# Moving stage four of the first two batches within their slots, in a Fourier-mixing and mixture-of-experts kernel

## The chip, the cores and the metric

The kernel runs on one core of a Trainium2 chip. The metric is the device time of one execution in microseconds; for the kernel before it is the median of three runs, 1559.63 us (1558.89 to 1561.95). A profiled execution of the same kernel spans 1579.1 us; all readings of the profile below are on that scale.

## The reference

Two blocks follow each other. The first takes 8 batches of 2496 tokens of 256 channels through a real Fourier transform along the tokens, multiplies by a complex filter and transforms back. The second sends each of the 19968 resulting tokens to the one of 8 experts with the highest gate logit; an expert is two matrix products with a relu between.

```python
X = np.fft.rfft(x, axis=1)
Y = X * (filt_r + 1j * filt_i)[None]
x = np.fft.irfft(Y, n=2496, axis=1).reshape(19968, 256)

logits = x @ w_gate
expert_idx = np.argmax(logits, axis=1)
gate_w = softmax(logits)[row, expert_idx]
for e in range(8):                      # rows of expert e
    h = np.maximum(x[rows] @ w1[e], 0.0)
    y[rows] = h @ w2[e]
out = gate_w[:, None] * y
```

## The kernel before

The length 2496 is 39 times 64, so each batch's transform is four products with small matrices: stage A (39 points, L342), stage B (64 points, L356) with the filter after it, stage C (64 points back, L382) and stage D (39 points back, L401 and L405), which is stage four. Between A and B, and between C and D, a batch goes through DRAM (`zd`, `ud`), as the axes change; only batch 0 stays on the chip and is turned by TensorE transposes instead. After D a batch is transposed (`turn_y`, L476), the logits are computed (L490) and transposed (L501), and a routing chain of small VectorE instructions finds the expert and the row of each token; GpSimd then scatters the rows to DRAM (L617). Once a batch is routed, a chain of small VectorE instructions (`tile_map`, L636 to L688) lists the expert tiles that are now full. Their work (transposes L750, first product L793 or L834, second product L851) fills the gaps between the Fourier steps.

The host program lays all steps of a slot on a scale from 0 to about 1 and emits them in that order; `slot(k)` has stages B and C of batch k, stage A of batch k + 1 and stage D with the routing of batch k - 1:

```python
def slot(k):
    steps, nch = [], len(CH)                       # nch = 6 chunks of up to 4 columns
    ...                                            # k == 0: batch 0 on the chip
    elif k < B:
        for f in range(0, NF + 4, 2):              # NF = 20
            at = f / (NF + 4)
            if f < NF:
                steps.append((at, lambda f=f: stage_b(k, f), ("z", k, f // 4) if f % 4 == 0 else None, 0.85))
            if f >= 4:
                steps.append((at + 0.01, lambda f=f: stage_c(k, f - 4), None, 0.85))
    if k + 1 < B:
        for c in range(nch):
            steps.append(((0.25 if k == 0 else 0.0) + 0.7 * c / nch, lambda c=c: stage_a(k + 1, c), ("x", k + 1, c), 0.43 * CH[c][1]))
    if k > 0:
        for c in range(nch + 3):
            at = 0.45 * c / (nch + 3) - 0.1 if k == 1 else 0.2 + 0.8 * c / (nch + 3)
            if c < nch and k == 1:
                steps.append((at - 0.05, lambda c=c: turn_u(c), None, 0.22 * CH[c][1]))
            if c < nch:
                steps.append((at, lambda c=c: stage_d(k - 1, c), ("u", k - 1, c) if k > 1 else "y", 0.43 * CH[c][1]))
            if c >= 3 and c % 2:
                steps.append((at + 0.01, lambda c=c: logits(k - 1, (c - 3) // 2), None, 0.9))
            if 1 <= c <= nch:
                steps.append((at + 0.03, lambda c=c: turn_y(k - 1, c - 1), None, 0.22 * CH[c - 1][1]))
            if c >= 3 and c % 2:
                later = at + (0.07 if k == 1 else 0.11)
                steps.append((later, lambda c=c: turn_logits(k - 1), None, 0.25))
                steps.append((later + 0.001, lambda c=c: sides.append(route(k - 1, (c - 3) // 2)), None, 0.0))
            if k == 1 and c == nch:
                steps.append((at, experts_pool, None, 0.0))
        steps.append((0.38 if k == 1 else 2.0, lambda: begin_route(k - 1), None, 0.0))
    return sorted(steps, key=lambda step: step[0])
```

`begin_route` appends the batch's tile map to `sides`, a queue of small work of which some instructions are emitted after each step. Stage B's multiplications by the filter are on VectorE; their final sum is on GpSimd for the first batches as long as `sides` is empty, else on VectorE:

```python
nc.vector.tensor_mul(ys, z2, ht[:, f:f + 2, :])                                   # L363
nc.vector.scalar_tensor_tensor(out=yw[:HP], in0=z2[HP:], scalar=-1.0, in1=fi, ...)  # L364
nc.vector.tensor_mul(yw[HP:], z2[:HP], fi)                                        # L365
if b == 0 or b < 3 and not sides:
    nc.gpsimd.tensor_tensor(ys, ys, yw, op=ALU.add)                               # L369
else:
    nc.vector.tensor_tensor(ys, ys, yw, op=ALU.add)                               # L372
```

Results in PSUM are evicted by VectorE or ScalarE (L228), whichever the host's own bookkeeping has free earlier. The routing chain has one instruction on ScalarE, the exponential (L527), in the midst of those on VectorE. All loads and stores other than the scatters are issued by SyncE, in the order in which they are emitted; inputs of the stages (`fin`) have 7 buffers, outputs that go to DRAM (`zo`, `uo`) share 4. A load of `u` is emitted once all of the batch's stage C is, and waits for its stores.

Of the kernel before, what the change touches and what calls it, by code (L numbers as in the profile page):

```python
# [118 lines left out]
def kernel(  # L119
# [216 lines left out]
    def stage_a(b, c):  # L336
        i0, n = CH[c]
        xt = ins.pop(("x", b, c))
        zo = sb.tile([TK, 4, D], F32, tag="st", name="zo", bufs=4)
        for j in range(0, n, 2):  # L340
            p = bank()
            mm(p[:TK, :], lhsT=tas, rhs=xt[:TP, j:j + 2, :], start=True, stop=True)  # L342
            evac(zo[:, j:j + 2, :], p[:TK, :].rearrange("p (t d) -> p t d", t=2), 512)
        for r, m, v in columns(zd[b], i0, n):
            move(v, zo[:r, m])
        if c == len(CH) - 1:
            mark(("a", b))

    def stage_b(b, f):
        c, j = divmod(f, 4)  # L350
        if b == 0:
            zi, j = outs.pop(("zi", f)), 0
        else:
            zi = ins["z", b, c] if j == 0 else ins.pop(("z", b, c))
        p = bank()
        mm(p, lhsT=tbs, rhs=zi[:, j:j + 2, :], start=True, stop=True)  # L356

        z2 = p.rearrange("p (i d) -> p i d", i=2)
        ys = outs["y", b, f] = sb.tile([P, 2, D], F32, tag="ys", name="ys", bufs=4)
        yw = (pro if b == 0 else sb).tile([P, 2, D], F32, tag="yw", name="yw", bufs=2)  # L360
        half, f1 = divmod(f, NF // 2)
        fi = ht[half * HP:(half + 1) * HP, NF + f1:NF + f1 + 2, :]
        nc.vector.tensor_mul(ys, z2, ht[:, f:f + 2, :])  # L363
        nc.vector.scalar_tensor_tensor(out=yw[:HP], in0=z2[HP:], scalar=-1.0, in1=fi, op0=ALU.mult, op1=ALU.mult)  # L364
        nc.vector.tensor_mul(yw[HP:], z2[:HP], fi)  # L365
        free["v"] = max(free["v"], now[0]) + 2.1

        if b == 0 or b < 3 and not sides:
            nc.gpsimd.tensor_tensor(ys, ys, yw, op=ALU.add)  # L369
            free["p"] = max(free["p"], free["v"]) + (1.4 if b else 0.0)  # L370
        else:
            nc.vector.tensor_tensor(ys, ys, yw, op=ALU.add)  # L372
            free["v"] += 0.7

    def stage_c(b, f):
        ys = outs.pop(("y", b, f))
        j = f % 4
        if j == 0:
            outs["u", b] = sb.tile([P, 4, D], F32, tag="st", name="uo", bufs=4)
        uo = outs["u", b]  # L380
        p = bank()
        mm(p, lhsT=tcs, rhs=ys, start=True, stop=True)  # L382
        evac(uo[:, j:j + 2, :], p.rearrange("p (i d) -> p i d", i=2), 512)
        if j == 2:
            f0 = f - 2
            move(ud[b][:, f0:f0 + 4, :], uo[:HP])
            move(ud[b][:, NF + f0:NF + f0 + 4, :], uo[HP:])
        if f == NF - 2:
            mark(("c", b))
# [42 lines left out]
    def turn_z(f):  # L432
        if f % 4 == 0:
            nc.scalar.copy(out=ht[HP:, f:f + 4], in_=ht[:HP, f:f + 4])
            free["s"] = max(free["s"], now[0]) + 1.1
        zi = outs["zi", f] = pro.tile([P, 2, D], F32, tag="zi", name="zi")
        p = bank().rearrange("p (i h d) -> p i h d", i=2, h=DH)
        for i in range(2):
            for h in range(DH):
                nc.tensor.transpose(p[:, i, h, :], zu["z"][:, h, f + i].rearrange("p c t -> p (c t)"), ident)  # L440
        evac(zi, p.rearrange("p i h d -> p i (h d)"), 2 * D)

    def first_c(f):
        ys = outs.pop(("y", 0, f))
        p = bank().rearrange("p (h i c t) -> p h i c t", h=DH, c=2, i=2)
        for i in range(2):
            for h in range(DH):
                mm(p[:, h, i].rearrange("p c t -> p (c t)"), lhsT=ys[:, i, h * P:(h + 1) * P],
                   rhs=tcs, start=True, stop=True)
        for h in range(DH):  # L450
            evac(zu["u"][:, h, :, :, f:f + 2], p[:, h].rearrange("p i c t -> p t c i"), D)

    def turn_u(c):
        i0, n = CH[c]
        ui = outs["ui", c] = pro.tile([P, 4, D], F32, tag="ui", name="ui")
        for j in range(0, n, 2):
            p = bank().rearrange("p (i h d) -> p i h d", i=2, h=DH)
            whole = i0 + j + 2 < NG
            for i in range(2):
                t0 = NB * (i0 + j + i)  # L460
                m = min(NB, N2 - t0)
                for h in range(DH):
                    nc.tensor.transpose(
                        p[:m * NS, i, h, :], zu["u"][:, h, t0:t0 + m].rearrange("p t c f -> p (t c f)"), ident)
                if not whole:
                    evac(ui[:m * NS, j + i, :], p[:m * NS, i].rearrange("p h d -> p (h d)"), D)
            if whole:
                evac(ui[:TK, j:j + 2], p[:TK].rearrange("p i h d -> p i (h d)"), 2 * D)

    def turn_y(b, c):  # L470
        yo = outs["o", b, c]
        for j in range(0, CH[c][1], 2):
            pt = bank().rearrange("p (i q) -> p i q", i=4)
            for i in range(2):
                for dh in range(DH):
                    nc.tensor.transpose(  # L476
                        pt[:, 2 * i + dh, :TP], yo[:, j + i, dh * P:(dh + 1) * P], ident[:TP, :TP]
                    )
            yt = yts[b, c, j] = sb.tile([P, 4, TP], F32, tag="yt", name="yt", bufs=4)
            evac(yt, pt[:, :, :TP], 4 * TP)  # L480
# [388 lines left out]
    def slot(k):  # L869

        steps, nch = [], len(CH)
        if k == 0:
            steps.append((0.4, load_rest, None, 0.0))
            for f in range(-2, NF + 2, 2):
                at = (f + 2) / (NF + 4)
                if 0 <= f < NF:
                    steps.append((at, lambda f=f: stage_b(k, f), None, 0.85))
                if f + 2 < NF:
                    steps.append((at + 0.01, lambda f=f: turn_z(f + 2), None, 0.44))
                if f >= 2:  # L880
                    steps.append((at + 0.02, lambda f=f: first_c(f - 2), None, 0.85))
        elif k < B:
            for f in range(0, NF + 4, 2):
# [7 lines that stand above are left out]
                steps.append(((0.25 if k == 0 else 0.0) + 0.7 * c / nch, lambda c=c: stage_a(k + 1, c), ("x", k + 1, c), 0.43 * CH[c][1]))  # L891
        if k > 0:
            for c in range(nch + 3):
                at = 0.45 * c / (nch + 3) - 0.1 if k == 1 else 0.2 + 0.8 * c / (nch + 3)
                if c < nch and k == 1:
                    steps.append((at - 0.05, lambda c=c: turn_u(c), None, 0.22 * CH[c][1]))
                if c < nch:
# [8 lines that stand above are left out]
                    steps.append((later + 0.001, lambda c=c: sides.append(route(k - 1, (c - 3) // 2)), None, 0.0))  # L906
                if k == 1 and c == nch:
                    steps.append((at, experts_pool, None, 0.0))
            steps.append((0.38 if k == 1 else 2.0, lambda: begin_route(k - 1), None, 0.0))
        return sorted(steps, key=lambda step: step[0])  # L910

    STEPS = [(0.0, lambda: load_filters(0), None, 0.0)]
# [5 lines left out]
    for k in range(B + 1):  # L918
        steps = slot(k)
# [3 lines left out]
    def begin_route(b):  # L923
        sides.append(after(b))
        left_t[0] = SLOT[b + 2] if b + 2 <= B else 1.0
# [201 lines left out]
```

## Time and profile before

| what | value |
|---|---|
| time, median of 3 | 1559.63 us |
| span of the profiled execution | 1579.1 us |
| TensorE busy (matmul) | 1519.2 us, 96% |
| VectorE, ScalarE, GpSimd busy | 740.5, 521.5, 668.2 us |
| mean DMA rate | 181 GB/s |
| TensorE in the chain that ended last | 79% |

The page counts a matmul as busy while it waits in a pipeline, so 96% is not 96% of the peak; what a stretch loses is seen from the pitch of its matmuls. A float32 product of 512 columns shows as two matmul records. A timeline line has start and duration in us, the engine, the line, the operation and its tiles, the count of merged instructions, and in brackets the idle time ahead of it and what ended it. A line of waits has the sum, the number and the longest wait.

### The profile page before, as it was taken

The numbers are of one execution on the slowest core, as the hardware profiler recorded it, in microseconds if no ns is written. First come the engines' busy times: TensorE is split into PE (matmuls) and PEld (weight loads), VectorE is DVE, ScalarE is ACT, GpSimd is POOL, SyncE is SP. The second block draws the span as 40 slices with busy tenths as digits, with TensorE's granted clock in tenths as the row PEclk, the third lists the DMA queues.
The fourth block names the chain that finished last, engine by engine and source line by source line (L and its number), as shares of the span: only waits on it lengthen the run. The fifth ranks groups of instructions, "written<-read, shape, count | busy, mean of one in ns | idle before, by whom it ended". The sixth has DMA issues, their size and how long they took to land.

```text
span 1579.1 us, 23774 instructions
## 1 busy us (share of the span) xinstructions
PE 1519.2 (96%) x7524; PEld 1200.9 (76%) x7524; DVE 740.5 (47%) x1911; ACT 521.5 (33%) x1059; POOL 668.2 (42%) x813
## 2 busy tenths in 40 slices
PE   7988898899999999999999999999999999999998
PEld 5533454777667876887777878888888889989997
DVE  4585557334485356365655554456424343430000
ACT  4433343233342324223332333223322232323333
POOL 3231232432544644344455554664455545641111
PEclk9998899999999999999999999999999999999999
DMA  9659896785695568444744463444445445575661
GB/s 229 177 159 279 258 287 206 227 246 179 187 301 188 157 158 273 138 121 165 203 143 121 137 189 104 138 138 165 161 155 188 136 145 165 183 254 170 176 183 38
DMA packets 118465, 285.18 MB, mean 181 GB/s; under 512 B 17411, under 2 KB 58380, under 8 KB 118341
## 3 DMA queue, kind: packets, MB, share of 16 engines
q1 hardware_dynamic: 99221, 240.32, 51.7%
q0 software_dynamic: 19120, 43.33, 7.9%
q8 instruction: 63, 1.03, 0.3%
q14 instruction: 61, 0.50, 0.1%
HBM read 203.58 MB, written 80.64 MB: 180 GB/s over the span
## 4 chain that ended last, share of the span: by engine, by line
PE 79%; issue 7%; DMA 7%; DVE 3%; POOL 1%; SPq 1%; ACT 1%; POOLq 0%; DVEq 0%; ACTq 0%
PE bank L851 30%; PE bank L793 23%; PE bank L401 4%; PE bank L356 4%; PE bank L342 4%; DMA out_dram<-ys,idt 3%; PE bank L834 3%; PE bank L382 3%; PE bank L476 2%; PE bank L750 2%; PE lt L490 2%; DVE hT L797 1%; DMA fin<-ud 1%; DMA ud<-uo 1%; DMA ht<-in_filt_dram 1%
## 5 line engine op out<-in xcount | busy, mean ns | idle before, releaser
L851 PE MATMUL bank<-w2t,hT 128*128 128x256 f32 x2240 | 498.8, 380 | 2.1 <-DMA w2t<-in_moe_w_dram 1.1
L851 PEld LDWEIGHTS bank<-w2t,hT 128*128 128x128 f32 x2240 | 421.1, 190 | 72.2 <-issue 13.1
L797 DVE TENSOR_TENSOR hT<-bank,hT 128x512 f32<-128x512 f32 (+1 forms) x504 | 300.0, 627 | 310.7 <-PE bank L793 171.0
L857 POOL DMA_INDIRECT out_dram<-ys,idt x161 | 159.3, 990 | 485.6 <-ACT ys L856 213.6
L617 POOL DMA_INDIRECT rows<-yo,row x176 | 175.4, 997 | 220.7 <-issue 68.5
L801 ACT ACTIVATE hT<-hT 128x1024 f32<-128x1024 f32 (+1 forms) x144 | 133.3, 957 | 339.1 <-DVE hT L797 333.1
L856 ACT ACTIVATE ys<-bank,gts 128x256 f32<-128x256 f32 x155 | 73.3, 475 | 398.9 <-PE bank L851 326.6
L793 PE MATMUL bank<-xT,w1t 128*128 128x256 f32 (+1 forms) x864 | 191.9, 358 | 0.9 <-DVE yw L365 0.9
L793 PEld LDWEIGHTS bank<-xT,w1t 128*128 128x128 f32 x864 | 152.5, 192 | 23.5 <-issue 5.8
L793 PE MATMUL bank<-sums,wsum 128*128 128x256 f32 (+1 forms) x576 | 138.4, 363 | 6.6 <-POOL sums L757 6.6
L834 PE MATMUL bank<-xT,w1t 128*128 128x128 f32 (+1 forms) x864 | 126.9, 302 | 0.9 <-DMA w1t<-in_moe_w_dram 0.6
L834 PEld LDWEIGHTS bank<-xT,w1t 128*128 128x128 f32 x864 | 116.4, 194 | 13.7 <-issue 6.9
L793 PEld LDWEIGHTS bank<-sums,wsum 128*128 128x128 f32 x576 | 102.0, 193 | 28.7 <-issue 10.5
L363 DVE TENSOR_TENSOR ys<-bank,ht 128x512 f32<-128x512 f32 x80 | 54.9, 687 | 95.1 <-PE bank L356 73.2
L768 POOL TENSOR_TENSOR wsum<-w1t 128x256 f32<-128x256 f32 x72 | 53.0, 736 | 106.4 <-PE bank L793 87.3
L744 DVE COPY idt<-xg 128x4 int32<-128x4 int32 (+2 forms) x63 | 18.2, 289 | 157.2 <-DMA out_dram<-ys,idt 138.3
L382 PE MATMUL bank<-ys,tcs 128*128 128x512 f32 x140 | 75.3, 620 | 6.0 <-DVE ys L372 4.2
L840 ACT ACTIVATE hT<-bank 128x128 f32<-128x128 f32 (+1 forms) x215 | 63.6, 301 | 52.5 <-PE bank L834 40.7
L342 PE MATMUL bank<-fin,tas 117*120 117x512 f32 x154 | 76.4, 615 | 0.0
L851 PE MATMUL bank<-w2s,hT 128*128 x336 | 76.0, 379 | 0.0
L356 PE MATMUL bank<-fin,tbs 128*128 128x512 f32 x140 | 75.8, 625 | 0.0
L401 PE MATMUL bank<-fin,tds 120*117 120x512 f32 x140 | 68.2, 609 | 7.8 <-DMA fin<-ud 7.5
(151 smaller groups left out, 1763.3 us busy)
## 6 DMA issues: line engine op xcount, KB each, us to landing
w1t<-in_moe_w_dram SPq DMA_DIRECT2D x126, 512.0 KB
w2t<-in_moe_w_dram SPq DMA_DIRECT2D x84, 512.0 KB
fin<-in_x_dram SPq DMA_DIRECT2D x39, 512.0 KB
fin<-zd SPq DMA_DIRECT2D x70, 256.0 KB
ud<-uo SPq DMA_DIRECT2D x70, 256.0 KB
zd<-zo SPq DMA_DIRECT2D x35, 480.0 KB
fin<-ud SPq DMA_DIRECT2D x35, 480.0 KB
xg<-rows SPq DMA_DIRECT2D x28, 544.0 KB
```

Of the source, the lines that this page charges most:

```text
L342: mm(p[:TK, :], lhsT=tas, rhs=xt[:TP, j:j + 2, :], start=True, stop=True)
L356: mm(p, lhsT=tbs, rhs=zi[:, j:j + 2, :], start=True, stop=True)
L382: mm(p, lhsT=tcs, rhs=ys, start=True, stop=True)
L401: mm(p[:TP, :], lhsT=tds, rhs=ui[:TK, j:j + 2, :], start=True, stop=True)
L617: sc = nc.gpsimd.indirect_dma_start(out=rowsd, out_offset=bass.IndirectOffsetOnAxis(ap=at, axis=0), in_=what, in_offset=None,)
L793: mm(q[:, v], lhsT=left[:, v * P:(v + 1) * P], rhs=right, start=True, stop=True)
L797: nc.vector.tensor_tensor(o, q, a, op=ALU.add)
L801: nc.scalar.activation(o.rearrange("p v r c -> p v (r c)"), q.rearrange("p v r c -> p v (r c)"), AF.Relu)
L834: mm(p[:, :m], lhsT=w1t[2 * i + g][:, dh, fh, v * P:(v + 1) * P], rhs=xts[i][:, dh, :m], start=(dh == 0), stop=(dh == DH - 1))
L851: mm(p[:, :D], lhsT=hs[i][k % 4 // 2][:, k // 4, k % 2, j * P:(j + 1) * P], rhs=w2, start=(k == 0), stop=(k == FT - 1))
L856: lambda: nc.scalar.activation(ys, p[:, :D], AF.Copy, scale=gate))
L857: nc.gpsimd.indirect_dma_start(out=out, out_offset=bass.IndirectOffsetOnAxis(ap=idt[i].bitcast(U32)[:, j, :], axis=0), in_=ys, in_offset=None,
```

## The change

Three numbers of the schedule change. Stage D of batch 0, with its transposes, logits and routing, is spread over 0.8 of slot 1 in place of 0.45; its tile map is queued at 0.73 in place of 0.38, after the routing. Stage D of batch 1 begins at 0.35 of slot 2 in place of 0.2. The later batches stay as they were. The purpose is to even out what the engines have to do within slot 1, and to give batch 1's data more time to come back from DRAM before stage D needs it. No computation is added or removed.

```diff
-                at = 0.45 * c / (nch + 3) - 0.1 if k == 1 else 0.2 + 0.8 * c / (nch + 3)
+                at = 0.8 * c / (nch + 3) - 0.1 if k == 1 else (0.35 if k == 2 else 0.2) + 0.8 * c / (nch + 3)
...
-            steps.append((0.38 if k == 1 else 2.0, lambda: begin_route(k - 1), None, 0.0))
+            steps.append((0.73 if k == 1 else 2.0, lambda: begin_route(k - 1), None, 0.0))
```

## The prediction

> **What bounds the kernel now.** I read the page's slices first: from slice 9 of 40 on TensorE shows 9 tenths nearly everywhere, before that 7 to 9. What it loses lies in the first fifth. The timeline of TensorE gives the slots (a slot k holds batch k's L356/L382 products): 1 at 68.35 to 121.30 us, 2 to 194.60, 3 to 267.50. The windows view of these, columns PE, PEld, DVE, ACT, POOL busy, clock, DMA share, GB/s:
> ```profile
> 68.35:121.30 52.95, 47.06 (x194) 22.82 (x193) 39.20 (x97) 21.26 (x44) 17.12 (x18) 0.94 0.66 178
> 121.30:194.60 73.30, 60.57 (x209) 30.30 (x208) 38.45 (x115) 26.85 (x55) 15.22 (x17) 0.86 0.87 270
> 194.60:267.50 72.90, 65.40 (x251) 36.61 (x251) 46.57 (x163) 28.44 (x59) 17.27 (x18) 0.91 0.77 227
> ...
> 340.00:400.00 60.00, 60.00 (x275) 44.00 (x273) 28.33 (x73) 21.52 (x48) 14.95 (x18) 1.00 0.71 214
> ```
> Slots 1 to 3 have holes and a clock below 1; from 340 us on there are none, because expert tiles fill them. TensorE's waits between 60 and 290 us name the holes:
> ```profile
> PE lt L490 <- ACT yt L228: 7.2, 4, 4.0
> PE bank L401 <- DMA fin<-ud: 6.8, 1, 6.8
> PE bank L793 <- POOL sums L757: 6.6, 1, 6.6
> PE bank L382 <- DVE ys L372: 4.2, 2, 3.3
> PE bank L750 <- DMA xg<-rows: 3.0, 2, 2.3
> PE rk L548 <- DVE oe L536: 2.1, 1, 2.1
> ```
> All eleven lines sum to 32.9 us. The idle time is not all: the timeline of TensorE around the end of slot 1 shows what follows a hole.
> ```profile
> 112.35 1.13 PE L382 MATMUL bank<-ys,tcs 128*128 128x512 f32 x2 [0.89 <-DVE ys L372]
> 116.74 2.05 PE L382 MATMUL bank<-ys,tcs 128*128 128x512 f32 x2 [3.27 <-DVE ys L372]
> 119.47 2.05 PE L382 MATMUL bank<-ys,tcs 128*128 128x512 f32 x2 [0.69 <-ACT uo L228]
> ...
> 129.07 1.02 PE L382 MATMUL bank<-ys,tcs 128*128 128x512 f32 x2
> 136.91 3.76 PE L401 MATMUL bank<-fin,tds 120*117 120x512 f32 x4 [6.82 <-DMA fin<-ud]
> ```
> A pair that takes 1.02 us elsewhere takes 2.05 after the hole.
>
> **How much is lost.** At full rate the timeline has a pitch of 0.86 us for a pair of L356, L382 or L342, 1.72 for four of L401, 0.80 for eight L476, 0.94 for sixteen L490; sixteen L834 or L851 take 3.45 in the chain. Slot 2: 10 L356 and 10 L382 17.2, eleven L342 pairs 9.5, stage four 9.7 (five fours 8.6, L405 1.1), L476 4.5, L490 2.6, small ones 1.4, one tile's L750 and L834 3.9; sum 48.8 of 73.3, lost 24.5. Of this 12.7 is listed idle time (6.82, 2.78, 0.20, 2.30, 0.62), the rest half rate. In the same way slot 1 has 43 of 53 (lost 10), slot 3 56.4 of 72.9 (lost 16.5). The hole before L793 at 282 us and its slow matmuls lose some 8.5. About 60 us in all; that is what this change can win from.
>
> **What the Trainium skill says.** "TensorE: Matmul & The Clock Gate", section "What's actually happening", has TensorE at half clock after about 3.4 us of idling and back after about as long busy. The trace agrees in size (2.05 for 1.02 us after 3.27 idle), so a hole cut to below 3 us should save its tail too. "Perfetto Trace Analysis", "Optimization Strategy", says that regimes with different limits may gain from interleaving: this is what the change does within a slot. "DMA: Bandwidth & Descriptors", "Two DMAs through the same engine are not ordered", has the issuing engine wait for a store's semaphore before it issues a load of the same bytes: the chain shows the store of `ud` from 125.07 for 6.99 us, the load from 132.20 for 4.66, and only then L401 at 136.91. No page puts a number on how SyncE's later loads suffer behind such a wait.
>
> **Part 1: batch 0's stage four over 0.8 of slot 1.** Nothing is added. L363, L364, L365 and, while routing work is pending, L372 cost VectorE 4 x 0.69 = 2.75 us for every L356 pair. Before, the first 20 us of slot 1 hold two such pairs and the next 22 eight (78.8 to 110.4), so 22 us of VectorE work and two routing chains of about 5 us (some 25 instructions at 0.2) fall into 30 us; hence the waits of 0.89 and 3.27. The order of the changed program puts three pairs ahead of the first routing chain (their L372 sum goes to GpSimd) and then one pair in 3 to 7 us of TensorE work. Walking through it, pairs at 0, 5.9, 10.1, 18, 22.6, 29.5, 33.3, 35.8, 38.6, 40.3 us, VectorE ends the last sum at about 46 where TensorE wants it at about 43. So 3 us of waiting stay of 4.2, and much of the 3.5 us of half rate goes: 3 us won. 1.7 us of transposes move from slot 0 into slot 1, which is neutral.
>
> **Part 2: batch 1's stage four 0.15 of a slot later.** In the old order L401 stands after 3 L356, 2 L342 steps and 1 L382 of slot 2; in the new one after 5, 4 and 3: 2 x 0.86 + 2 x 1.72 + 2 x 0.86 = 6.9 us more work ahead of it, against a hole of 6.82. But the order on SyncE now puts two `x` loads and a `z` load among the last stores of `ud`, and the zo and uo buffers (four together) are released by stores that stand behind the `ud` load, so ScalarE may be held up. I leave 3 us of the hole and half its 3 us tail: 5 us won.
>
> The end of slot 2 changes more. Here ScalarE's stream is:
> ```profile
> 166.29 0.23 ACT L228 COPY lg<-bank 117x64 f32<-117x64 f32 x1
> 170.94 0.26 ACT L527 ACTIVATE ex<-ex 117x64 f32<-117x64 f32 x1 [4.42 <-DVE ex L526]
> 171.10 0.57 ACT L228 COPY zo<-bank 120x512 f32<-120x512 f32 x1
> 171.57 1.00 ACT L228 COPY yt<-bank 128x468 f32<-128x468 f32 x2
> ```
> The exponential waits for VectorE, which is busy with the 22 small instructions of the tile map (166.92 to 170.3), and the evictions behind it wait too; TensorE then waits 2.78 for yt, with a tail of about 2.5. SyncE's zd stores wait as well, and the rows of the first tile come late (2.30 and 0.62 idle, and L834's sixteen take 6.66 instead of 3.45). In the new order the tile map is split by an L356 pair, one more pair stands before the logits, and the first tile moves into slot 3. Of 2.8 + 2.5 + 2.9 + 3.2 = 11.4 us I expect 3.5 to stay: 8 won.
>
> **Slots 3 and 4.** Both tile maps of batch 1 stand in one block ahead of the exponential in the new order too, so the 3.99 wait and its 4 us tail stay. The 2.11 at L548 with its 4 us tail may be halved, as that chain has expert results ahead of it: 3 won. The last routing chain of slot 3 stands a little earlier against the first 512-row tile, which should shorten the 6.63 us that L793 waits for POOL's sums behind eight scatters: 2 won. From slot 5 on both programs have the same TensorE order, so nothing there should move.
>
> **Sum.** 3 + 5 + 8 + 3 + 2 = 21 us. I take back 9 for transfers: the three slots move 9.43 + 19.82 + 16.55 = 45.8 MB in 0.66 x 52.95 + 0.87 x 73.3 + 0.77 x 72.9 = 155 us of DMA busy time, while TensorE's full-rate work in them is 148. When 199 us shrink, DMA is the next limit, and z, x and u loads will come late here and there. Net -12: 1559.6 - 12 = 1548 us.
>
> **The rivals.** (a) Transfers take it all. Slot 2 has a DMA share of 0.87 already, and hurried slots find u and z not landed. For it: long stretches at 9 tenths. Against it: TensorE shows no wait on zd or x after 60 us, and the DMA strip has empty stretches while SyncE is blocked. Time: 1556 to 1562. (b) The tile lost as filler in slot 2 costs more than the later start saves: the end of slot 2 is then a bare chain of transposes, logits and transposes, with evictions of 0.36 to 1.0 us between. Against it: such waits are 0.2 to 0.5 now. Time: 1560 to 1568. (c) The holes nearly all close and DMA keeps pace at the 400 GB/s that the strip reaches for some slices: 25 us or more won, 1530 to 1535.
>
> **Range and chances.** The step from 60 us lost to 21 won is a sum of five guesses, each good to perhaps half of itself, and the 9 taken back could be 0 or 20. So 1534 to 1561. Over 2% needs 31 us, more than half of all that is lost: 0.06. Over 2% slower would need holes that are not there now, for unchanged work: 0.02. Within 2%: 0.92.
>
> **What would show it.** Right: slot 1's waits on L372 below 4 us, the wait of L401 on `ud` at 3 us or less, slot 2 under 62 us with the first L834 in slot 3, the wait on yt near 172 us gone and the one near 250 still there, L548's idle time halved, slots from 5 on of the same length. Wrong: L401 still waiting 6 us or more (then the chain through SyncE moved along with the work), or new waits on zd or x (rival a), or slot 3 longer by as much as slot 2 is shorter.

## The result and the profile after

| | before | after | ratio, 95% interval |
|---|---|---|---|
| time, median of 6 and 6 | 1559.88 us | 1553.41 us (1550.66 to 1556.43) | 0.9956 [0.9942, 0.9970] |
| the same pair on a second chip, median of 17 and 9 | 1573.25 us | 1563.23 us | 0.9941 [0.9921, 0.9962] |

The change saves 6.5 us on the first chip and 10.0 us on the second, 0.4 to 0.6%. The forecast was 1548 us within 1534 to 1561, a gain of 12 us, with most weight on "within 2%". Chips and executions differ by more than the change does (the kernel before took 1558.9 to 1575.6 us in five comparisons, and its profile shown in the prediction is of an execution of 1580.8 us), so each ratio below is taken on one chip.

The windows view of the kernel after, slots 1, 2 and 3, then slot 5 to the end, with the same columns as the one of before (PE, PEld, DVE, ACT, POOL busy, clock, DMA share, GB/s):
```profile
64.97:116.12 51.15, 46.74 (x209) 23.45 (x208) 38.91 (x91) 21.89 (x44) 12.33 (x13) 1.00 0.70 182
116.12:176.11 59.99, 50.35 (x188) 22.91 (x189) 39.80 (x121) 24.45 (x50) 14.31 (x15) 0.94 0.92 275
176.11:257.79 81.68, 68.44 (x270) 39.87 (x270) 48.43 (x168) 29.04 (x61) 29.88 (x31) 0.92 0.85 264
...
411.46:1552.70 1141.24, 1128.86 (x5888) 952.09 (x5886) 517.18 (x1266) 362.82 (x731) 528.45 (x657) 1.00 0.54 166
```
Slot 2 is short now and slot 3 long. TensorE's waits of the kernel after between 60 and 290 us (sum, number, longest) answer to the six shown of before:
```profile
PE bank L750 <- DMA xg<-rows: 7.6, 2, 5.1
PE bank L401 <- DMA fin<-ud: 7.0, 2, 4.9
PE bank L382 <- DVE ys L372: 3.0, 2, 1.6
...
PE lt L490 <- ACT yt L228: 1.0, 2, 0.5
```
The wait on yt has nearly gone, as have those on POOL's sums and at L548. The waits on `ud` are in sum as large as ever, and those on the rows of the first tiles have grown. The timeline of TensorE of the kernel after shows where they stand:
```profile
139.23 3.73 PE L401 MATMUL bank<-fin,tds 120*117 120x512 f32 x4 [4.94 <-DMA fin<-ud]
...
169.22 1.43 PE L490 MATMUL lt<-yt,wg 128*32 128x234 f32 x12 [0.42 <-ACT yt L228]
...
254.00 1.94 PE L750 MATMUL bank<-ident,xg 128*128 128x128 f32 x8 [5.10 <-DMA xg<-rows]
```
The wait near 172 us was 2.78 and is 0.42; the first L834 stands at 183.57, in slot 3. But L401 still waits 4.94 us, and its four take 3.73 where 1.88 is usual, so the whole tail is there too.

For where the time went, two executions profiled on the same chip in the same comparison are used. They are 11.1 us apart in span, near to the 10.0 us of the medians there.

| stretch | before, us | after, us | difference | of it moved work |
|---|---|---|---|---|
| up to slot 1 | 64.97 | 61.80 | -3.2 | -1.7 transposes, now in slot 1 |
| slot 1 | 52.95 | 52.21 | -0.7 | +1.7 |
| slot 2 | 70.40 | 62.20 | -8.2 | -3.9, the first tile, now in slot 3 |
| slot 3 | 73.82 | 78.50 | +4.7 | +3.9 |
| slot 4 | 159.38 | 155.97 | -3.4 | |
| slot 5 to the end | 1143.28 | 1143.02 | -0.3 | |

Net of moved work slot 1 wins 2.4 us, slots 2 and 3 together 3.5, slot 4 3.4. All executions of the change agree on the pattern, not on the tenth: in the first profile after, slot 2 is 2.2 us shorter and slot 3 is 3.2 longer than in this one.

### The profile page after: what moved, and what is told of

Read it like the earlier page. It is cut to its first block, busy times and chain, and to the rows that moved or that the text cites. A ratio compares the mean times of both kernels' runs of the same rounds, so it can differ in the third digit from the quotient of the medians.

```text
span 1552.7 us, 23781 instructions
## 1 busy us (share of the span) xinstructions
PE 1500.8 (97%) x7524; PEld 1192.7 (77%) x7524; DVE 749.1 (48%) x1916; ACT 519.9 (33%) x1053; POOL 669.6 (43%) x814
## 3 DMA queue, kind: packets, MB, share of 16 engines
q8 instruction: 63, 1.03, 0.3%
## 4 chain that ended last, share of the span: by engine, by line
PE 78%; DMA 9%; issue 7%; DVE 4%; SPq 0%; ACT 0%; POOL 0%; POOLq 0%; DVEq 0%; ACTq 0%
PE bank L851 31%; PE bank L793 23%; PE bank L401 4%; PE bank L342 4%; PE bank L356 4%; DMA out_dram<-ys,idt 3%; PE bank L382 3%; PE bank L834 3%; PE bank L750 2%; PE bank L476 2%; DMA fin<-in_x_dram 2%; PE lt L490 1%; DMA fin<-ud 1%; DMA ud<-uo 1%; DVE hT L797 1%
## 5 line engine op out<-in xcount | busy, mean ns | idle before, releaser
L793 PE MATMUL bank<-xT,w1t 128*128 128x256 f32 (+1 forms) x864 | 190.3, 356 | 0.0
L793 PEld LDWEIGHTS bank<-xT,w1t 128*128 128x128 f32 x864 | 151.6, 190 | 21.9 <-issue 4.3
L793 PE MATMUL bank<-sums,wsum 128*128 128x256 f32 (+1 forms) x576 | 135.5, 358 | 0.0
L834 PEld LDWEIGHTS bank<-xT,w1t 128*128 128x128 f32 x864 | 116.2, 193 | 15.6 <-issue 9.5
L834 PE MATMUL bank<-xT,w1t 128*128 128x128 f32 (+1 forms) x864 | 126.6, 302 | 1.5 <-DMA w1t<-in_moe_w_dram 1.5
L793 PEld LDWEIGHTS bank<-sums,wsum 128*128 128x128 f32 x576 | 100.4, 190 | 19.6 <-issue 9.6
L401 PE MATMUL bank<-fin,tds 120*117 120x512 f32 x140 | 69.4, 617 | 8.5 <-DMA fin<-ud 7.4
L342 PE MATMUL bank<-fin,tas 117*120 117x512 f32 x154 | 73.5, 595 | 2.4 <-DMA fin<-in_x_dram 2.0
L356 PE MATMUL bank<-fin,tbs 128*128 128x512 f32 x140 | 73.2, 606 | 1.6 <-issue 1.4
```

Of the source, the lines that this page charges most:

```text
L401: mm(p[:TP, :], lhsT=tds, rhs=ui[:TK, j:j + 2, :], start=True, stop=True)
L793: mm(q[:, v], lhsT=left[:, v * P:(v + 1) * P], rhs=right, start=True, stop=True)
L834: mm(p[:, :m], lhsT=w1t[2 * i + g][:, dh, fh, v * P:(v + 1) * P], rhs=xts[i][:, dh, :m], start=(dh == 0), stop=(dh == DH - 1))
```

## The experiments

### The kernel before again

> The kernel before, unchanged, for a second profile: the profiled execution of before took 1580.8 us while its timed ones took 1559 to 1562. Theory 'odd profile': this profile spans about 1558 and its slot 5 begins near 420 us, not 433.6, so that the stage lengths of before and after can be compared at the 6.5 us that were measured. Theory 'profiling itself costs this kernel 20 us': it spans 1575 to 1580 again. Time 1558 to 1562 in both.

Measured: 1574.7 us against 1575.59 for the same kernel, 1.0004 [0.9987, 1.0021]: a ratio of this comparison is good to about 0.2%. Neither theory holds as it stands: on this chip the timed executions are as long as the profiled one. Its slots 1 to 3 take 52.95, 70.84 and 72.20 us, its waits on yt sum to 7.1 and on `ud` to 5.7.

A second profile of it, unchanged, gave the column "before" of the table above:

> The kernel before, for a profile on the same chip as the changed kernel's. Both theories: 1558 to 1580 by the chip. If chips differ and not executions, its profile lies within 3 us of the timed runs of before on this chip, and the difference of the two kernels' profiles is that of their times.

Measured: a span of 1564.8, with waits on yt of 8.8, on `ud` of 7.2 and on POOL's sums of only 0.8, where the profile in the prediction has 6.6 and the run above 6.2. The wait before L793 thus comes and goes between executions of one and the same kernel.

### The change alone again

> The changed kernel, unchanged, on whatever chip this call gets; its two parts alone gave 0.9997 and 0.9989 of the time before, together 0.9956 on another chip. If the parts only work together (part 1 alone ends slot 1 earlier and then waits longer for u; part 2 alone takes that wait), the ratio is 0.994 to 0.997 here too. If the earlier chip favoured the change, it is 0.998 or more here, the sum of the parts.

Measured: 1563.23 against 1573.25, 0.9941 [0.9921, 0.9962]. Its waits sum to 6.4 on `ud` (longest 4.5), 4.3 on yt and 2.6 on the rows; in the first profile after it was 7.0, 1.0 and 7.6. The last two change places; the first stays. The ratio is at the low end of the range that was said to show that the parts work only together; the next two runs take that up again.

### Part 1 alone

```diff
-    ... else (0.35 if k == 2 else 0.2) + 0.8 * c / (nch + 3)
+    ... else 0.2 + 0.8 * c / (nch + 3)
```


> Part 1 alone: batch 0's stage four over 0.8 of slot 1 and its tile map at 0.73; batch 1's stays at 0.2. Theory A (the gain is in slot 2: more work ahead of the u load, and the first tile out of its end) has it at 1556 to 1559. Rival B (the gain is VectorE evened out in slot 1, the u load's chain just moves along) has it at 1551 to 1554.

Measured: 1574.68 us, 0.9997 [0.9983, 1.0010]: nothing. The waits of this run:
```profile
PE lt L490 <- ACT yt L228: 9.6, 4, 6.5
PE bank L401 <- DMA fin<-ud: 8.9, 2, 7.4
```
In slot 1 L372 is not waited for in this execution, though a ranking product (L548) waits 1.98 us for VectorE; in the changed kernel, with the same order in slot 1, the waits on L372 sum to 3.0. Slot 1 takes 53.28 us with the 1.7 us of moved transposes in it, so some 1.4 us are won. The wait of L401 on `ud` in slot 2 is 7.4 us, longer than any in the kernel before, but the slot itself is no longer for it (69.79 us, and 70.84 in the kernel before on this chip). What takes the gain back stands later: slot 3 takes 75.02 us for 72.20, with a wait on yt of 6.5, and the slots from 5 on 1147.8 for 1144.0.

### Part 2 alone

```diff
-    at = 0.8 * c / (nch + 3) - 0.1 if k == 1 else ...
+    at = 0.45 * c / (nch + 3) - 0.1 if k == 1 else ...
...
-    steps.append((0.73 if k == 1 else 2.0, ...))
+    steps.append((0.38 if k == 1 else 2.0, ...))
```


> Part 2 alone: batch 1's stage four at 0.35, batch 0's as before. Theory A: 1553 to 1556, with the wait of L401 on u at 5 us or less. Rival B: 1559 to 1563, the wait of L401 still near 7. If the parts add up, the gains of this run and of part 1 alone sum to 6.5 us.

Measured: 1572.58 us, 0.9989 [0.9978, 1.0001], 3.0 us if anything. The waits:
```profile
PE lt L490 <- ACT yt L228: 6.4, 2, 6.2
PE bank L750 <- DMA xg<-rows: 5.8, 2, 4.5
...
PE bank L401 <- DMA fin<-ud: 3.1, 2, 2.4
```
Here the wait on `ud` is down to 2.4 us, near the 3 of the prediction: L401 has 6.9 us more of work ahead of it, and the first load of `u` is issued 13.3 us after the slot's start, where the kernel before has 9.5 to 10.9 in three executions. Slot 2 takes 67.84 us. Slot 3 keeps its long wait on yt (6.2), and so does slot 4 its wait on sums (5.2).

In the medians neither part alone does what both do: 0.9997 and 0.9989 against 0.9941. That the parts need each other is not shown by this. From slot 5 on, where none of these edits was meant to act, the two runs take 1147.8 and 1147.3 us, 3.8 and 3.3 more than the kernel before on this chip (1144.0), while the kernels before and after take 1141 to 1146 everywhere. Their TensorE order differs there: slot 6 has 816 matmul records in place of 800, and the rest of the span 16 fewer. With these 3.8 and 3.3 us given back, the parts' 0.9 and 3.0 us would be 4.7 and 6.3, an estimate that sums to 11, as much as the 10.0 of both together. Whether that order costs the 3 us was not tested by itself: of the kernels further down that have it, the one on this chip takes 1146.7 us from slot 5 on, two on other chips 1139.7 and 1139.9.

### Later still

```diff
-    ... (0.35 if k == 2 else 0.2) + 0.8 * c / (nch + 3)
+    ... (0.5 if k == 2 else 0.2) + 0.8 * c / (nch + 3)
```


> The changed kernel with batch 1's stage four at 0.5 of slot 2 in place of 0.35. If the u load's chain has a fixed length after the last stage C of slot 1, the work put ahead of L401 (about 7 us more) takes up its remaining 4.9 us: wait under 1 us, time 1549 to 1552. If ScalarE held up by zo and uo buffers moves the work along with the chain, the wait stays at 3 to 5 us and the barer end of slot 2 costs: 1553 to 1558.

Measured: 1561.41 us against 1575.59, 0.9908 [0.9889, 0.9926]. The wait of L401 in slot 2 is 0.36 us and the slot 57.95, though in slot 3 L401 now waits 3.60. More distance does close the hole, though the held-up ScalarE of the other theory shows as well: an L356 in slot 2 waits 2.75 us for `zo`. The 0.15 of the change is too short a step, all the more once slot 1 is quicker.

### Who holds `u` back: batch 1's stores of `u` issued by ScalarE

```diff
-    def move(o, i):
-        moves[1].append(lambda: nc.sync.dma_start(out=o, in_=i))
+    def move(o, i, queue=None):
+        moves[1].append(lambda: (queue or nc.sync).dma_start(out=o, in_=i))
...
-            move(ud[b][:, f0:f0 + 4, :], uo[:HP])
-            move(ud[b][:, NF + f0:NF + f0 + 4, :], uo[HP:])
+            move(ud[b][:, f0:f0 + 4, :], uo[:HP], nc.scalar if b == 1 else None)
+            move(ud[b][:, NF + f0:NF + f0 + 4, :], uo[HP:], nc.scalar if b == 1 else None)
```
The TensorE order is that of the changed kernel. What this looks into is SyncE's timeline around the start of slot 2, first in the kernel before (slot 2 begins at 121.31 us), then in the kernel after (116.12):
```profile
117.53 7.98 SPq L301 DMA_DIRECT2D ud<-uo  x6
132.20 0.36 SPq L334 DMA_DIRECT2D fin<-ud  x1
```
```profile
112.44 1.06 SPq L322 DMA_DIRECT2D fin<-in_x_dram  x2
...
117.14 1.18 SPq L301 DMA_DIRECT2D ud<-uo  x2
120.58 0.33 SPq L322 DMA_DIRECT2D fin<-in_x_dram  x1
121.55 5.16 SPq L301 DMA_DIRECT2D ud<-uo  x4
134.19 0.36 SPq L334 DMA_DIRECT2D fin<-ud  x1
```
Before, the last six stores follow each other; after, they stand behind and among loads of x and z. The pair at 117.14 had its data evicted by about 111.5. The last four begin at 121.55, and the first `u` load is issued at 134.19, when they have landed. Meanwhile ScalarE waits for the same stores, as its timeline shows:
```profile
129.52 1.07 ACT L228 COPY zo<-bank 120x512 f32<-120x512 f32 x2 [9.04 <-DMA ud<-uo]
```

> The changed kernel with batch 1's stores of u issued by ScalarE in place of SyncE; TensorE's order unchanged. In the changed kernel the first of the last six stores is evicted at 111.5 us but issued at 117.1, behind loads of z and x and a wait for zd, and the u load lands at 139.2. If SyncE's order makes the u load late: stores issued 4 to 6 us earlier, the wait of L401 on u from 4.5 to 4.9 down to 1 or less, 3 to 6 us won with the half-rate tail. If the transfers themselves are saturated there: the wait stays over 3 us, time within 2 us of the changed kernel.

Measured: 1547.02 us against 1558.88, 0.9923 [0.9901, 0.9945]. The timeline of this run, of both issuing queues and TensorE, slot 2 beginning at 112.99:
```profile
113.42 1.11 ACTq L301 DMA_DIRECT2D ud<-uo  x2
...
117.71 3.74 PE L342 MATMUL bank<-fin,tas 117*120 117x512 f32 x4 [2.83 <-DMA fin<-in_x_dram]
...
123.17 0.36 SPq L334 DMA_DIRECT2D fin<-ud  x1
...
133.48 1.88 PE L401 MATMUL bank<-fin,tds 120*117 120x512 f32 x4
```
The last two stores of `u` begin 0.43 us after the slot's start, the `u` load 10.2 us after it instead of 18.1 (134.19 - 116.12), and L401 runs at 1.88 us without a wait. Over the runs, in us after the start of slot 2 (the stores from the single instructions of the traces; "TensorE ready" is the start of L401 less its wait):

| kernel | last store of `u` issued | first load of `u` issued | TensorE ready for L401 | L401 waits |
|---|---|---|---|---|
| before | 3.8 | 10.9 | 8.8 | 6.8 |
| part 1 alone | 3.8 | 10.4 | 8.5 | 7.4 |
| part 2 alone | 7.3 | 13.3 | 16.3 | 2.4 |
| after | 10.1 | 18.1 | 18.2 | 4.9 |
| after, second execution | 9.2 | 16.8 | 17.4 | 4.5 |
| stores issued by ScalarE | 0.9 | 10.2 | 20.5 | 0 |

From the last store to the load it is 6.0 to 9.3 us in all of them, the longest in the last one. This settles the cause of the hole: it was the place of the stores in SyncE's order, not the time the bytes need. Slot 2 takes 55.14 us in place of 59.99. The Trainium skill, "DMA: Bandwidth & Descriptors", "Issuing engines are not separate DMA queues", says that a second issuing engine saves only the time to initiate a transfer. Measured here the load comes 7.9 us earlier (6.6 against the second execution), since the first engine's order has waits in it.

The whole gain over the change is less sure: the interval of 0.9923 overlaps with both of the change's, 0.9956 and 0.9941. Two likely reasons are in sight. In slot 3, where batch 2's stores are still SyncE's, L401 now waits 4.0 us for `u` in place of 2.0:
```profile
PE bank L401 <- DMA fin<-ud: 4.0, 1, 4.0
```
And L342 waits 2.83 us for x, in a stretch at half rate, while the DMA strip of 110 to 145 us, in 40 slices, is full from end to end. That of the kernel after comes first, then that of this run:
```profile
DMA  6016989999999999999999999510349999999999
```
```profile
DMA  9969699999999999999999999999999999999999
```
The mean rates there are 262 and 322 GB/s, and over slot 2 275 and 302. What is won is more bytes in the same time.

### Who holds yt back: the exponential moved to the end of its chain

```diff
-        nc.scalar.activation(ex, ex, AF.Exp)            # L527, and the sum of ex at L540
...                                                      # both taken out of the chain's midst
+        nc.scalar.activation(ex, ex, AF.Exp)
+        nc.vector.tensor_reduce(sd, ex, axis=AX.X, op=ALU.add)
         rk = psr.tile(...)                              # put just ahead of this
```


> The changed kernel with the routing's exponential (and the sum after it) emitted just ahead of the ranking products, when VectorE has the chain behind it, in place of in the chain's midst. Theory 'ScalarE held by the exponential': the waits of L490 on yt (0.5 to 4 us, with tails) vanish, and about 3 to 6 us are won over the changed kernel. Rival 'transfer bound': the waits turn into waits on xg, u or z of the same length, and the time is within 1 us of the changed kernel's.

Measured: 1583.08 us, 1.0076 [1.0050, 1.0101], 20 us slower than the change. No wait on yt is left in the whole span, so ScalarE's exponential was what held the evictions. But slot 5 to the end takes 1167 us in place of 1143, and over the whole span L490 waits 10.3 us for VectorE's `rks`, 5.1 in the change. Up to slot 5 nothing is won either (411.9 us, in the change 410.7). The TensorE order of the later slots changed as well, so which of the two costs the 20 us is argued, not shown. The next kernel does the same for batches 0 to 2 alone and has the TensorE order of the changed kernel.

> The changed kernel with the exponential moved behind the chain's VectorE work for batches 0 to 2 alone; TensorE's order is that of the changed kernel, instruction for instruction. Theory 'the wait has its own cost': no wait of L490 on yt over 1 us in slot 3, and 3 to 6 us won over the changed kernel (ratio to before 0.990 to 0.992). Rival 'the next wait takes its place' (the changed kernel's first profile had 0.5 us on yt but 5.1 on xg, its second 4.3 on yt and none on xg): the wait on xg at the end of slot 3 is 4 us or more, and the ratio stays at 0.993 to 0.996.

Measured: 1549.32 us against 1558.88, 0.9937 [0.9913, 0.9961]: no more than the change itself has. Its timeline of TensorE (line numbers are five higher here, L755 is L750):
```profile
245.21 1.00 PE L490 MATMUL lt<-yt,wg 128*32 128x234 f32 x12 [2.83 <-DVE rks L557]
249.86 1.94 PE L755 MATMUL bank<-ident,xg 128*128 128x128 f32 x8 [2.21 <-DMA xg<-rows]
```
The wait on yt is gone, and the one on VectorE just behind it is 2.83 us where the change has 1.5. The rows are waited for 2.21 us here, less than the 4 that the rival named, and 3.85 at the start of slot 3.

### A tile's rows expected later

The host's bookkeeping supposes that the load of an expert tile's rows (`xg`) lands 9 us after its issue; with 13, other work is put ahead of the tile's transposes (L750).
```diff
-            when["x", i] = now[0] + 9.0
+            when["x", i] = now[0] + 13.0
```


> The changed kernel with a tile's transposes emitted 13 us (of the emitter's clock) after its rows' load in place of 9. If the new waits of L750 on xg (2.6 and 5.1 us) are the load's latency of 7 to 9 us against too little work emitted in between, they vanish and 4 to 8 us are won. If the loads are late because the transfers are saturated, the waits stay or move to w1 and u: within 2 us of the changed kernel.

Measured: 1563.69 us against 1573.25, 0.9945 [0.9927, 0.9963], as the change. No wait on the rows is left; these are longer than in the change (6.4 to 7.0, none and 1.0 to 4.3):
```profile
PE bank L401 <- DMA fin<-ud: 10.3, 2, 5.7
PE bank L793 <- POOL wsum L769: 5.3, 1, 5.3
PE lt L490 <- ACT yt L228: 5.3, 2, 4.2
```

### What helps, together

> The same move of the exponential on the kernel with batch 1's stage four at 0.5 (which alone had 0.9908). Own cost: 0.987 to 0.989. Next wait takes its place: 0.990 to 0.993.

Measured: 1542.48 us against 1558.88, 0.9902 [0.9886, 0.9917]. That is the 0.9908 of the later start, so the exponential adds nothing that can be measured to that either. Its last stretch, slot 5 to the end, is one of those named above. With ScalarE's issuing of the stores added as well:

> Batch 1's stage four at 0.5, the exponential moved for batches 0 to 2, and batch 1's stores of u issued by ScalarE: the three edits that each lost nothing, together. If the gains add (ratios 0.991 for 0.5 with or without the exponential's move, and 2 to 4 us for the stores), 0.986 to 0.989 of the time before. If the stores only help where L401 stands early, and at 0.5 the transfers are the limit at the start of slot 2, 0.990 or more: new waits on x or z of 3 us or more there.

Measured: 1540.50 us against 1558.94, 0.9886 [0.9861, 0.9911], the lowest ratio of all and clear of the change's own intervals, though on another chip. It is not clear of the 0.9902 and 0.9908 without these stores, so what they add here is not shown. Its slot 2, in the windows view:
```profile
115.35:167.98 52.63, 47.41 (x189) 22.35 (x188) 39.79 (x121) 25.07 (x50) 13.91 (x14) 1.00 0.99 326
```
The mean clock is 1.00 and the DMA share 0.99: the DMA engines have no idle time left in this slot, though TensorE waits for x only 1.8 us there, below the 3 that would have spoken for transfers as the limit.

## Why the prediction was right, and where its terms were off

**Slot 1, 3 us won: right.** The eight pairs of L356 stand from 88.8 to 110.4 us and not from 78.8, a slip that changes nothing in the sum. Won are 2.4 us in the pair, and the wait on L372 fell to 3.0, where 3 of 4.2 were said to stay. What the sum left out is that an earlier start of slot 2 finds SyncE no further on; this comes under the next head.

**The hole before L401, 5 us won: the step that failed.** "I leave 3 us of the hole and half its 3 us tail" became 4.94 and 4.53 us in two executions, with all of the tail (3.73 for 1.88). Against 5.7 to 6.8 in the kernel before 1 to 2 us are won, and new small waits in the same stretch of the first profile after (1.37, 0.87 and 0.70) take them back: about 0 in place of 5. The 6.9 us of work ahead of L401 were counted rightly. What was too small is the delay of the load that goes with it: the sum allowed about 3 us, and the load of `u` is issued 7.2 us later after the slot's start (18.1 for 10.9). That is near to the sign that the prediction gave for being wrong, a chain through SyncE that moves along with the work. The prediction had named the cause, two x loads and a z load among these stores, and only the size was off. Part 2 alone, with this same order on SyncE, has 2.4 of the 7.2 us. The rest came with part 1: slot 2 starts 3.6 us earlier than in part 2 alone (116.12 for 119.69), but SyncE, which first waits for stores of `zd`, comes to the z loads ahead of these stores at nearly the same time (111.28 for 111.80). The run with ScalarE as issuer, where no wait is left, shows that the order was the whole hole; that an earlier slot 1 made it worse is read from single executions.

**The end of slot 2, 8 us won: right as a mechanism.** Slot 2 is 59.99 and 62.20 us in two executions, against the 62 of the test; the tile has moved, the wait on yt is 0.42. Whether its rows are in time varies: in the first profile L750 waits 2.55 us and L834's sixteen take 5.38 in slot 3, so that the part of the 8 for the tile's late rows was moved, not won; in the second L750 does not wait and the sixteen take 3.72.

**Slot 3, 3 us won: wrong in sign.** Net of the moved tile it is 0.8 us longer. L548's wait, which was to be halved, has gone; but of three executions of the kernel before only two have it (2.1 and 2.8), so it was no fixed cost. "The 3.99 wait and its 4 us tail stay" holds in one execution (4.3 on yt) and not in the other, where yt costs 0.54 and the rows of the next tile 5.10. The two experiments on these waits show why neither is worth its length: remove yt, and VectorE's `rks` and the rows are waited for; remove the rows, and yt, `ud` and wsum are.

**Slot 4, 2 us won: 3.4, in this pair by luck.** The wait on POOL's sums that the term rested on is at most 0.7 us in both executions of the change and 6.6, 6.2 and 0.8 in three of the kernel before, so it may well have been shortened. But the pair has 0.8 and 0.7 of it, and TensorE's listed waits in the slot sum to 4.0 and 3.8 us. What differs is the mean clock, 0.98 and 1.00, which is an estimated 3 us of the 159.

**Slots from 5 on: right,** 1143.28 and 1143.02 us.

**The 9 us taken back.** For slots 2 and 3 the sum had 5 + 8 + 3 - 9 = 7 us, the pair shows 4.3 - 0.8 = 3.5. With the hole at 0 and the other terms kept, 8 + 3 - 3.5 = 7.5 would be what was taken back. This is a remainder, which holds the errors of those terms too, so that the 9 comes near is luck, and the total owes to it in part that it lies near 1548. The 9 was taken for transfers at their limit; what the runs show in the changed kernel is waits that change places, with the order on SyncE behind the largest. Once the stores are off SyncE, transfers come nearer: L342 waits 2.83 us for x.

**The rivals.** Transfers taking all (1556 to 1562) and the lost filler (1560 to 1568) are both above what was measured on that chip, and holes that nearly all close (1530 to 1535) below it; even the best version stands at 1540.5. Slot 3 longer by as much as slot 2 is shorter, a sign of being wrong, came half true: +4.7 against -8.2, of which 3.9 is moved work.

## What to carry to other kernels

When work is moved away from a wait, ask whether the wait's cause moves with it: a store stands in its issuing engine's order behind everything emitted earlier, and waits there for what that waits for (here a store whose data was ready at 111.5 us was issued at 117.1). A wait seen in a profile is worth its length only if nothing else is due just behind it, so take one away by itself before counting it. Two parts of a change can meet in one chain: the load of `u` was issued 10.4 us after the slot's start with the first part alone, 13.3 with the second and 18.1 with both. And before the times of parts are added up, look whether a stretch that none of them was meant to touch has changed: here it moved by more than either part won.

## What the runs showed of the hardware

Issuing ten stores from a second engine brought the load that depends on them 7.9 us earlier after the slot's start, at an unchanged order of TensorE, and raised the DMA rate over the slot from 275 to 302 GB/s.

Short holes can slow TensorE too, and the length of one hole does not decide. The Trainium skill, "TensorE: Matmul & The Clock Gate", "What's actually happening", puts the idle window at about 3.4 us and says that it runs free. Two lines agree with that, the first from slot 3 of the kernel after, the second from slot 2 of part 2 alone:
```profile
196.78 2.81 PE L401 MATMUL bank<-fin,tds 120*117 120x512 f32 x4 [2.04 <-DMA fin<-ud]
199.38 1.90 PE L834 MATMUL bank<-xT,w1t 128*128 128x256 f32 x4
```
```profile
138.37 1.95 PE L401 MATMUL bank<-fin,tds 120*117 120x512 f32 x4 [2.43 <-DMA fin<-ud]
140.15 1.02 PE L356 MATMUL bank<-fin,tbs 128*128 128x512 f32 x2
```
After 2.04 us idle the four L401 take 2.81 for the usual 1.88, and four L834 1.90 for the 1.03 that they take at 191.36. After 2.43 us idle, which is longer, four L401 take 1.95 and what follows is at full rate. That a hole below 3 us "should save its tail too" was therefore too hopeful: it may.
